# A Mamba-2 scan ahead of a hash-routed expert layer: other load pieces, another order of steps, three experts' weights on chip

## The chip, the cores and the metric

The kernel runs on one core of one Trainium2 chip. Its engines are TensorE (PE, with its weight loads as PEld), VectorE (DVE), ScalarE (ACT), GpSimd (POOL) and SyncE (SP), which here only issues transfers. The metric is the device time of one execution in microseconds, lower is better. All arithmetic is float32, apart from small tables of the routing.

## What is computed

Four batches of eight heads are scanned in chunks, and the result, 3072 tokens of 256 values, goes through one of eight experts, chosen by a hash of the token's id.

```python
# scan: x (4, 8, 768, 32), a (4, 8, 768), B and C (4, 8, 768, 16)
cum = np.cumsum(np.log(a_chunk), axis=-1)
M = einsum('bhin,bhjn->bhij', Cc, Bc) * exp(cum_i - cum_j) * causal
y = einsum('bhij,bhjd->bhid', M, xc) + einsum('bhin,bhnd->bhid', Cc, state) * exp(cum)
state = exp(sum(la)) * state + sum_j Bx * exp(cum_last - cum_j)
# experts: 3072 tokens of 256, w1 (8, 256, 1024), w2 (8, 1024, 256)
e = token_id * 2654435761 % 8
out[token] = relu(y[token] @ w1[e]) @ w2[e]
```

## The kernel before

The kernel has a prologue, a scan and an expert stage. The scan is one loop over 24 tiles `gc` of 128 tokens (L523), six tiles to a batch, and each tile holds two steps of 64 tokens, so a batch has 12 steps `k`. The order on every engine of prologue and scan is the program's (`tc.manual_schedule`, L78); in the expert stage a planner orders the work.

For a tile, `grams(gc)` (L451) multiplies B with C on PE and VectorE masks the product into `m` (L463); `outputs(gc)` (L467) adds the part from the state (`cp` by `up`, L476) and the part inside the chunk (`m` by `x`, L485), ScalarE copies it out (L489), and SyncE stores it to the scratch tensor `y_tokens` (L490). The products of a tile are made one tile ahead of its outputs.

While a batch's tiles run, the next batch is prepared by pieces, one after each tile's outputs. `rows(b, i)` (L357) scales B (i = 0) or C (i = 1) with the decays, on GpSimd for batches 1 to 3. `put_steps(b)` (L364) stores B's rows to the DRAM scratch `b_steps`; `get_steps(b)` (L367) reads them back in another layout as `bs`, by two transfers that wait for the store. `turn_b(b)` and `turn_c(b)` (L398, L404) transpose the rows on PE (L395) and copy them out of PSUM; `turn_c` makes `ct`, `cp` and the two masked copies `ce`. `states(b, half)` (L419) multiplies `bs` with `x` on PE (L431) and runs the recurrence over the steps on VectorE (L436, L438); `blocks` (L441) spreads the states into `up` on GpSimd. For batch 0 there is no trip through DRAM: `turn_steps(0)` (L375) transposes on PE instead.

For batch 1 the pieces come after tiles 0 to 4 (rows and store after 0, `turn_b` and `get_steps` after 1, `turn_c` after 2, the two halves of `states` after 3 and 4), and rows of batch 2 after tile 5. For batches 2 and 3, `turn_b` comes after tile 6 or 12, `turn_c` after 7 or 13, `states` after 8, 9 or 14, 15, and the rows and the store of batch 3 after tile 10. B and C of a batch arrive by `load_bc` (L87, two buffers), x by `load_x` (L94, two transfers, three buffers); batches 0 and 1 are asked for in the prologue, batch 2 after tiles 3 and 4, batch 3 after tiles 6 and 7. All of these, and the stores of y, stand in SyncE's one queue in program order.

The routing's many small VectorE operations are a generator (`routing`, L182): three of its parts run in the prologue (`next(todo)`, L306, L312, L499), the others one after each tile from tile 7. `spin` (L155) is PE work whose result nobody reads.

In the expert stage each expert has 416 slots. `gather` (L586) fetches token rows by an indirect transfer that GpSimd issues, `turn_x` transposes them, `up` and `down` (L607, L614) are the two products, and the results are scattered to the output. An expert's two weights take 1 MB each; `load_w` (L112) has NWB = 4 buffers. Experts 0 and 1 are loaded from ScalarE's queue after tiles 13 and 17, expert 2 from SyncE's at the end of the scan (L559), expert 3 by L625, later ones when an expert's buffers come free.

Of the kernel before, what the change touches and what calls it, by code (L numbers as in the profile page):

```python
# [20 lines left out]
def kernel(  # L21
# [21 lines left out]
    NCH = NT // P  # L43
    DP = DM // P
    FP = F // P
    NWB = 4
    CAP = 416
    KT = -(-CAP // P)
    LR = CAP - (KT - 1) * P
# [41 lines left out]
                              in_=src[b].rearrange("h (p r) n -> p h (r n)", r=RS))  # L91
        bcs[b] = t

    def load_x(b):  # L94

        t = aload.tile([P, G, NU, D], F32, name="x_t", bufs=3)
        for q in range(2):
            nc.sync.dma_start(out=t[q * HL:(q + 1) * HL].rearrange("j h k d -> j (h k) d"),
                              in_=x[b, q * G:(q + 1) * G].rearrange("h s d -> (h s) d").rearrange("(c j) d -> j c d", j=HL))
        xs[b] = t  # L100

    tok_h = dataclasses.replace(moe_token_ids.tensor, shape=list(moe_token_ids.tensor.shape))
    tok = route.tile([NCH, P, 2], I32)
# [2 lines left out]
    load_x(0)  # L106
    load_bc(1)
    load_x(1)

    w1s, w2s = {}, {}  # L110

# [43 lines left out]
    def spin(moving, n=1):  # L155

        t = ps_y.tile([P, 2, 512], F32, name="y_ps")
        for _ in range(n):
            nc.tensor.matmul(out=t[:, 0, 0:moving.shape[-1]], lhsT=ident[0:moving.shape[0]], rhs=moving,
                             start=True, stop=True)  # L160
# [141 lines left out]
    tot = cum[:, :, RS - 1]  # L302
    rel_ps = ps_t.tile([P, 512], F32, name="tp")
    nc.tensor.matmul(out=rel_ps[0:NR, 0:BH], lhsT=rel_w.rearrange("p k r -> p (k r)"), rhs=tot, start=True, stop=True)
    todo = iter(routing())
    next(todo)  # L306
    rel = apre.tile([NR, BH, RS], F32)
    nc.vector.tensor_tensor(out=rel, in0=cum, in1=rel_ps[0:NR, 0:BH].unsqueeze(2).to_broadcast([NR, BH, RS]), op=OP.add)
    fac = apre.tile([NR, 2, BH, RS], F32)
    nc.scalar.activation(fac[:, 0], rel, AF.Exp, scale=-1.0)  # L310
    nc.scalar.activation(fac[:, 1], rel, AF.Exp)
    next(todo)  # L312
    spin(flat(cum), 4)

    totx = apre.tile([NR, BH, NS], F32)
    step = const.tile([P, NB, NU], F32)
# [17 lines left out]
    def steps():  # L334
        step_ps = ps_t.tile([P, 512], F32, name="tp")
        for b in range(NB):
            nc.tensor.matmul(out=step_ps[:, b * NU:(b + 1) * NU],
                             lhsT=totx[:, b * H:(b + 1) * H].rearrange("p h n -> p (h n)"), rhs=step_w,
                             start=True, stop=True)
        nc.scalar.activation(step.rearrange("p b k -> p (b k)"), step_ps[:, 0:NB * NU], AF.Exp)  # L340
# [16 lines left out]
    def rows(b, i, eng):  # L357

        t = abat.tile([NR, RS, P], F32, name="rows", bufs=2)
        eng.tensor_tensor(out=t.rearrange("p r (h n) -> p h r n", h=H), in0=bcs[b][:, i],  # L360
                          in1=fac[:, i, b * H:(b + 1) * H].unsqueeze(3).to_broadcast([NR, H, RS, NS]), op=OP.mult)
        rws[b, i] = t

    def put_steps(b):  # L364
        nc.sync.dma_start(out=b_dram[b].rearrange("(p r) n -> p r n", r=RS), in_=rws[b, 0])

    def get_steps(b):  # L367

        t = abat.tile([P, NU, HL], F32, name="bs")
        for q in range(2):  # L370
            nc.sync.dma_start(out=t[q * HL:(q + 1) * HL],
                              in_=b_dram[b].rearrange("(k j) (q n) -> q j k n", j=HL, q=2)[q])
        bss[b] = t
# [24 lines left out]
    def turn_b(b):  # L398
        bt = abat.tile([P, NR, RS], F32, name="bt")
        for rs, v in turned(b, 0):  # L400
            nc.scalar.activation(bt[:, :, rs], v, AF.Copy)
        bts[b] = bt.rearrange("p (k c) r -> p k (c r)", c=RU)

    def turn_c(b, first=False):  # L404
        ct = abat.tile([P, NR, RS], F32, name="ct", bufs=1)
        ce = abat.tile([P, 2, NR, RS], F32, name="ce")
        for rs, v in turned(b, 1):
            nc.scalar.activation(ce[:, 0, :, rs], v, AF.Identity, scale=par[:, 0:1])
            if first:
                nc.vector.tensor_scalar(out=ce[:, 1, :, rs], in0=v, scalar1=par[:, 1:2], scalar2=None, op0=OP.mult)  # L410
            else:
                nc.scalar.activation(ce[:, 1, :, rs], v, AF.Identity, scale=par[:, 1:2])
            nc.scalar.activation(ct[:, :, rs], v, AF.Copy)
        cp = abat.tile([P, NU, HL], F32, name="cp")
        nc.gpsimd.tensor_tensor(out=cp, in0=ct.rearrange("p (k c) r -> p k (c r)", c=RU),
                          in1=step[:, b].unsqueeze(2).to_broadcast([P, NU, HL]), op=OP.mult)
        ces[b], cps[b] = ce.rearrange("p e (k c) r -> p e k (c r)", c=RU), cp
# [33 lines left out]
    def grams(gc):  # L451

        b, c = divmod(gc, R)
        gram = ps_g.tile([P, 2, 512], F32, name="gram")
        for u in range(2):
            for r in range(G):
                q, g = divmod(r, 2)
                rr = slice(32 * r, 32 * r + 32)
                nc.tensor.matmul(out=gram[q * HL:(q + 1) * HL, g, u * P:(u + 1) * P],  # L459
                                 lhsT=bts[b][rr, 2 * c + u], rhs=ces[b][rr, :, 2 * c + u],  # L460
                                 start=True, stop=True)
        m = awork.tile([P, 2, 2, 2, HL], F32, name="m")
        nc.vector.tensor_tensor(out=m.rearrange("p g u e i -> p g (u e i)"), in0=gram[:, :, 0:2 * P],  # L463
                                in1=causal.rearrange("p (g x) i -> p g (x i)", g=2), op=OP.mult)
        ms[gc] = m
# [24 lines left out]
        nc.sync.dma_start(out=y_dram[gc * P:(gc + 1) * P, :], in_=y_sb.rearrange("p q d -> p (q d)"))  # L490

    rows(0, 0, nc.vector)
    rows(0, 1, nc.vector)
    heads()
    steps()
    spin(ones, 2)
    turn_b(0)
    spin(ones, 2)
    next(todo)  # L499
    turn_c(0, True)  # L500
    turn_steps(0)
    grams(0)
    states(0, 0)
    blocks(0, 1, 2, nc.vector)
    blocks(0, 2, UH + 1, nc.gpsimd)

    def prepare(nb, what):
        if nb >= NB:
            return
        if what == "rows":  # L510
            rows(nb, 0, nc.gpsimd)
            put_steps(nb)
            rows(nb, 1, nc.gpsimd)
        elif what == "b":
            turn_b(nb)
            get_steps(nb)
        elif what == "c":
            turn_c(nb)
        else:
            states(nb, what)  # L520
            blocks(nb, *((1, UH + 1), (UH + 1, NU))[what], nc.gpsimd)

    for gc in range(NCH):  # L523
        b, c = divmod(gc, R)
        nb = b + 1
        if gc + 1 < NCH:
            grams(gc + 1)
        outputs(gc)
        if gc == 0:
            states(0, 1)  # L530
            blocks(0, UH + 1, NU, nc.gpsimd)
        if gc > 6:
            next(todo, None)
        if b == 0:
            if c in (0, 1):
                prepare(1, ("rows", "b")[c])
            elif c == 2:
                prepare(1, "c")
            elif c == 3:
                prepare(1, 0)  # L540
                load_bc(2)
            elif c == 4:
                prepare(1, 1)
                load_x(2)
            else:
                prepare(2, "rows")
        elif c < 4:
            prepare(nb, ("b", "c", 0, 1)[c])
            if c == 0 and nb + 1 < NB:
                load_bc(nb + 1)  # L550
            if c == 1 and nb + 1 < NB:
                load_x(nb + 1)
        elif c == 4:
            prepare(nb + 1, "rows")
        if gc in (13, 17):
            load_w((gc - 13) // 4, nc.scalar)
    for _ in todo:
        pass
    load_w(2, nc.sync)  # L559
    scan_order.__exit__(None, None, None)  # L560
    a_ctx.close()

# [51 lines left out]
    def down(e, f):  # L614
        if f == 0:
            oP[e] = ps_o.tile([P, DP, 512], F32, name="o_ps")
        h = hT.pop((e, f))
        for j in range(DP):
            nc.tensor.matmul(out=oP[e][:, j, 0:CAP], lhsT=w2s[e][:, f, j * P:(j + 1) * P], rhs=h,  # L619
                             start=(f == 0), stop=(f == FP - 1))  # L620
        if f == FP - 1:
            if e + NWB < E:
                load_w(e + NWB, nc.sync)
            if e == 0:
                load_w(NWB - 1, nc.sync)  # L625
            op = oP.pop(e)
            oT[e] = mwork.tile([P, DP, CAP], F32, name="oT")
            for j in range(DP):
                if j % 2 == 0:
                    nc.scalar.activation(oT[e][:, j], op[:, j, 0:CAP], AF.Copy)  # L630
                else:
                    nc.vector.tensor_copy(out=oT[e][:, j], in_=op[:, j, 0:CAP])
# [19 lines left out]
    for u in range(E * FP + LAG):  # L652
        e, f = divmod(u, FP)
        if e < E:
            up(e, f)
        if u >= LAG:
            down(*divmod(u - LAG, FP))
        if f >= FP - KT and e + 1 < E:
            turn_x(e + 1, f - (FP - KT))
            if e + 2 < E:  # L660
                gather(e + 2, f - (FP - KT))
        if LAG < f <= LAG + KT and 0 < e < E:
            turn_o(e - 1, f - LAG - 1)
# [74 lines left out]
```

## Time and profile before

| what | us |
|---|---|
| median of 3 runs | 337.86 (337.04 to 339.86) |
| the profiled execution, its own time | 338.07 |
| its span, first to last instruction | 336.3 |
| PE busy in it | 285.5 (85%) |
| POOL, DVE, ACT busy in it | 100.7, 99.8, 53.9 |
| first products of the expert stage begin at | 125.1 |

Times within the execution count from the first instruction. An entry of the timeline or of the chain gives its start, its length and its engine; "<-" in brackets names what ended the idle time before it. The granted clock is TensorE's clock as a share of 2.4 GHz, so 0.50 is 1.2 GHz. SPq, ACTq and POOLq are the sequencers that issue transfers.

### The profile page before, as it was taken

How to read it: one execution, taken by the hardware profiler on the slowest of the kernel's cores; microseconds unless marked ns; L12 is line 12 of the kernel's file. 1: busy time of each engine (PE TensorE's matmuls, PEld its weight loads, DVE VectorE, ACT ScalarE, POOL GpSimd, SP SyncE). 2: the span in 40 equal slices, each digit the busy share in tenths (PEclk: the TensorE clock that was granted, in tenths of full speed). 3: DMA queues.
4: the chain of work that ended last, by engine and by line, in shares of the span. 5: the costliest groups of instructions: out<-in, count | busy, mean ns of one | idle time of the engine just before them, and what ended most of it. 6: DMA issues, size and time to landing. Idle time of an engine off the chain costs nothing.

```text
span 336.3 us, 6038 instructions
## 1 busy us (share of the span) xinstructions
PE 285.5 (85%) x2507; PEld 180.8 (54%) x2507; DVE 99.8 (30%) x215; ACT 53.9 (16%) x116; POOL 100.7 (30%) x114
## 2 busy tenths in 40 slices
PE   6786975678968149999999999999999999999930
PEld 5765855567756125555555555555555555555510
DVE  4642245486784010212212221211211311211110
ACT  4301424003301001011201101102111111111110
POOL 6136181260410372220530531531621301302240
PEclk9957595555769558999999999999999999999975
DMA  7992496963855792043154154244200000000110
GB/s 120 154 117 63 98 159 135 206 133 96 285 175 176 241 368 76 16 160 125 55 168 125 62 165 125 78 144 135 69 20 16 30 2 16 31 0 16 35 48 1
DMA packets 55936, 35.64 MB, mean 106 GB/s; under 512 B 34464, under 2 KB 51898, under 8 KB 55909
## 3 DMA queue, kind: packets, MB, share of 16 engines
q1 hardware_dynamic: 50468, 24.51, 32.4%
q0 software_dynamic: 2816, 6.56, 6.1%
q10 hardware_dynamic: 2624, 4.19, 3.8%
q8 instruction: 20, 0.33, 0.5%
q14 instruction: 8, 0.06, 0.1%
HBM read 27.78 MB, written 7.73 MB: 106 GB/s over the span
## 4 chain that ended last, share of the span: by engine, by line
PE 51%; issue 20%; DMA 12%; DVE 7%; POOL 6%; ACT 2%; SPq 0%; POOLq 0%; ACTq 0%; DVEq 0%
PE h_ps L610 17%; PE o_ps L619 16%; DMA out_dram<-o_sb,idx_out 6%; PE gram L459 4%; POOL out_dram L580 3%; PE y_ps L485 3%; PE tp L395 2%; DMA xg<-y_tokens,idx_in 2%; PE y_ps L476 2%; PE tp L431 2%; PE xt_ps L598 2%; DVE st L438 1%; DMA bs<-b_steps 1%; POOL rows L360 1%; DMA a_t<-in_a_dram 1%
## 5 line engine op out<-in xcount | busy, mean ns | idle before, releaser
L610 PE MATMUL h_ps<-xT,w 128*128 128x416 f32 x256 | 101.8, 522 | 0.3 <-issue 0.3
L619 PE MATMUL o_ps<-hT,w 128*128 128x416 f32 x256 | 102.1, 518 | 0.0
L619 PEld LDWEIGHTS o_ps<-hT,w 128*128 128x128 f32 x256 | 47.5, 190 | 40.1 <-issue 36.3
L580 POOL DMA_INDIRECT out_dram<-o_sb,idx_out x32 | 31.2, 975 | 114.1 <-ACT o_sb L641 95.8
L610 PEld LDWEIGHTS h_ps<-xT,w 128*128 128x128 f32 x256 | 47.1, 194 | 32.3 <-issue 31.1
L575 POOL DMA_INDIRECT xg<-y_tokens,idx_in x32 | 32.0, 1001 | 54.9 <-issue 21.0
L605 DVE TENSOR_SCALAR hT<-h_ps 128x416 f32<-128x416 f32 x32 | 18.9, 592 | 74.4 <-PE h_ps L610 74.4
L599 DVE COPY xT<-xt_ps 128x256 f32<-128x256 f32 (+1 forms) x32 | 12.0, 374 | 77.2 <-PE xt_ps L598 76.7
L603 ACT ACTIVATE hT<-h_ps 128x416 f32<-128x416 f32 x32 | 16.5, 517 | 99.0 <-PE h_ps L610 81.5
L459 PE MATMUL gram<-ce,bt 32*64 32x128 f32 x384 | 24.3, 372 | 1.9 <-issue 1.9
L463 DVE TENSOR_TENSOR m<-gram,causal 128x512 f32<-128x512 f32 x24 | 16.5, 687 | 25.2 <-PE gram L459 25.2
L485 PE MATMUL y_ps<-x_t,m 64*64 64x32 f32 x768 | 20.8, 254 | 2.6 <-DVE m L463 2.0
L598 PE MATMUL xt_ps<-ident,xg 128*128 128x128 f32 (+1 forms) x64 | 12.6, 280 | 12.0 <-issue 10.1
L485 PEld LDWEIGHTS y_ps<-x_t,m 64*64 64x64 f32 x768 | 20.7, 180 | 3.8 <-DVE m L463 3.0
L598 PEld LDWEIGHTS xt_ps<-ident,xg 128*128 128x128 f32 (+1 forms) x64 | 8.5, 148 | 25.2 <-issue 22.1
L446 POOL TENSOR_TENSOR up<-st,own 128x640 f32<-128x640 f32 (+1 forms) x8 | 13.1, 1643 | 26.2 <-DVE st L438 26.2
L489 ACT ACTIVATE y_sb<-y_ps 128x256 f32<-128x256 f32 x24 | 9.2, 383 | 65.2 <-PE y_ps L485 63.1
L459 PEld LDWEIGHTS gram<-ce,bt 32*64 32x64 f32 x384 | 15.4, 181 | 5.8 <-issue 4.8
L476 PE MATMUL y_ps<-up,cp 64*64 64x128 f32 x176 | 14.2, 365 | 3.1 <-issue 1.3
L641 ACT ACTIVATE o_sb<-ot_ps 128x256 f32<-128x256 f32 x16 | 6.1, 383 | 60.2 <-PE ot_ps L638 60.2
L431 PE MATMUL tp<-x_t,bs 64*32 64x64 f32 x352 | 10.5, 290 | 6.0 <-DMA bs<-b_steps 6.0
L395 PE MATMUL tp<-ident,rows 96*128 96x96 f32 x64 | 10.3, 328 | 5.5 <-POOL rows L360 5.5
(122 smaller groups left out, 178.6 us busy)
## 6 DMA issues: line engine op xcount, KB each, us to landing
w<-in_moe_w_dram SPq DMA_DIRECT2D x12, 1024.0 KB, 5.5
w<-in_moe_w_dram ACTq DMA_DIRECT2D x4, 1024.0 KB, 5.9
x_t<-in_x_dram SPq DMA_DIRECT2D x8, 384.0 KB, 9.1
y_tokens<-y_sb SPq DMA_DIRECT2D x24, 128.0 KB, 3.2
bc<-in_B_dram SPq DMA_DIRECT2D x4, 384.0 KB, 6.8
bc<-in_C_dram SPq DMA_DIRECT2D x4, 384.0 KB, 6.1
b_steps<-rows SPq DMA_DIRECT2D x3, 384.0 KB, 3.3
bs<-b_steps SPq DMA_DIRECT2D x6, 192.0 KB, 3.7
```

The costliest lines, as they stand in the source:

```text
L395: nc.tensor.transpose(out=v[:, :, r], in_=t[:, r0 + r], identity=ident[0:NR, 0:NR])
L431: nc.tensor.matmul(out=tp[32 * r:32 * r + 32, i * PW:(i + 1) * PW], lhsT=bs[w, k, 32 * g:32 * g + 32], rhs=xb[w, 2 * g:2 * g + 2, k], star ...
L459: nc.tensor.matmul(out=gram[q * HL:(q + 1) * HL, g, u * P:(u + 1) * P], lhsT=bts[b][rr, 2 * c + u], rhs=ces[b][rr, :, 2 * c + u], start=Tr ...
L463: nc.vector.tensor_tensor(out=m.rearrange("p g u e i -> p g (u e i)"), in0=gram[:, :, 0:2 * P], in1=causal.rearrange("p (g x) i -> p g (x ...
L476: nc.tensor.matmul(out=y_ps[u * HL:(u + 1) * HL, q, 0:P], lhsT=cps[b][w, k], rhs=ups[b][w, k].rearrange("p g x -> p (g x)"), start=True, s ...
L485: nc.tensor.matmul(out=y_ps[u * HL:(u + 1) * HL, q, h * D:(h + 1) * D], lhsT=m[w, g, u, e], rhs=xs[b][w, h, k], start=(k == 0 and h == 0), ...
L575: nc.gpsimd.indirect_dma_start(out=dst, out_offset=None, in_=y_dram[:], in_offset=bass.IndirectOffsetOnAxis(ap=idx, axis=0), bounds_check= ...
L580: st = nc.gpsimd.indirect_dma_start(out=out[:], out_offset=bass.IndirectOffsetOnAxis(ap=idx, axis=0), in_=src, in_offset=None, bounds_chec ...
L598: nc.tensor.transpose(out=tp[:, i, 0:r], in_=g[0:r, i * P:(i + 1) * P], identity=ident[0:r, 0:r])
L605: nc.vector.tensor_scalar_max(out=o, in0=i, scalar1=0.0)
L610: nc.tensor.matmul(out=hp, lhsT=w1s[e][:, i, f * P:(f + 1) * P], rhs=xT[e][:, i], start=(i == 0), stop=(i == DP - 1))
L619: nc.tensor.matmul(out=oP[e][:, j, 0:CAP], lhsT=w2s[e][:, f, j * P:(j + 1) * P], rhs=h, start=(f == 0), stop=(f == FP - 1))
```

## The change

- `load_x` takes a piece number: x of batches 2 and 3 is asked for in four pieces of two heads, each by two transfers (one a head, 96 KB instead of 384 KB), after tiles 1 to 4 (batch 2) and 6 to 9 (batch 3). Batches 0 and 1 stay whole.
- B and C of batch 2 are asked for at the end of the prologue's loads, those of batch 3 after tile 6.
- B's rows of batch 1 are made ahead of the tile loop, behind `blocks(0, 2, ...)` on GpSimd, and C's rows after tile 0. For batches 2 and 3 B's rows are made after tile 4 or 9, ahead of that tile's `blocks`, and the store and C's rows come after tile 5 or 10.
- In the prologue, the routing's first part comes behind the decays, its second ahead of `turn_c`, its third behind the first `grams`; `steps` and `turn_b(0)` come ahead of `rows(0, 1)`; two of the spins go and one is shortened.
- In `turn_c` for batch 0, ScalarE copies `ct` out of PSUM, and both `ce` are made from that copy in SBUF, in two halves of positions, one mask on ScalarE and one on VectorE.
- NWB is 3. Expert 2 is loaded from ScalarE's queue in the expert stage, behind the second `up`; the loads at L559 and L625 go.

```diff
-    NWB = 4
+    NWB = 3
+    def load_x(b, i=None):
+        if i in (None, 0):
+            xs[b] = aload.tile([P, G, NU, D], F32, name="x_t", bufs=3)
+        for h in range(*((0, H, G) if i is None else (2 * i, 2 * i + 2))):
+            q, g = divmod(h, G)
+            n = G if i is None else 1
+            nc.sync.dma_start(out=xs[b][q * HL:(q + 1) * HL, g:g + n].rearrange("j h k d -> j (h k) d"),
+                              in_=x[b, h:h + n].rearrange("h s d -> (h s) d").rearrange("(c j) d -> j c d", j=HL))
     load_x(1)
+    load_bc(2)
...
-    todo = iter(routing())
-    next(todo)
     rel = apre.tile([NR, BH, RS], F32)
...
     nc.scalar.activation(fac[:, 1], rel, AF.Exp)
+    todo = iter(routing())
     next(todo)
-    spin(flat(cum), 4)
+    spin(flat(cum), 3)
...
         for rs, v in turned(b, 1):
             nc.scalar.activation(ct[:, :, rs], v, AF.Copy)
+            if not first:
+                for e in range(2):
+                    nc.scalar.activation(ce[:, e, :, rs], v, AF.Identity, scale=par[:, e:e + 1])
+        for p in range(0, NR, NR // 2) if first else ():
+            ps = slice(p, p + NR // 2)
+            nc.scalar.activation(ce[:, 0, ps], ct[:, ps], AF.Identity, scale=par[:, 0:1])
+            nc.vector.tensor_scalar(out=ce[:, 1, ps], in0=ct[:, ps], scalar1=par[:, 1:2], scalar2=None, op0=OP.mult)
...
     rows(0, 0, nc.vector)
+    steps()
+    turn_b(0)
     rows(0, 1, nc.vector)
     heads()
-    steps()
-    spin(ones, 2)
-    turn_b(0)
-    spin(ones, 2)
     next(todo)
     turn_c(0, True)
     turn_steps(0)
     grams(0)
+    next(todo)
     states(0, 0)
     blocks(0, 1, 2, nc.vector)
     blocks(0, 2, UH + 1, nc.gpsimd)
+    rows(1, 0, nc.gpsimd)
     for gc in range(NCH):
...
+        b, c = divmod(gc - (b == 0), R)
+        nb = max(b, 0) + 1
+        after = nb + 1
+        if nb == NB:
+            continue
+        if gc == 0:
+            put_steps(1)
+            rows(1, 1, nc.gpsimd)
+        elif c == 0:
+            turn_b(nb)
+            get_steps(nb)
+            if nb == 2:
+                load_bc(3)
+        elif c == 1:
+            turn_c(nb)
+        elif c == 2:
+            states(nb, 0)
+            blocks(nb, 1, UH + 1, nc.gpsimd)
+        elif c == 3:
+            states(nb, 1)
+            if after < NB:
+                rows(after, 0, nc.gpsimd)
+            blocks(nb, UH + 1, NU, nc.gpsimd)
+        elif c == 4 and after < NB:
+            put_steps(after)
+            rows(after, 1, nc.gpsimd)
+        if after < NB and gc > 0 and c < 4:
+            load_x(after, c)
         if gc in (13, 17):
             load_w((gc - 13) // 4, nc.scalar)
...
-    load_w(2, nc.sync)
...
-            if e == 0:
-                load_w(NWB - 1, nc.sync)
...
             up(e, f)
+        if u == 1:
+            load_w(NWB - 1, nc.scalar)
```

## Rows read from the trace of the kernel before

**Rows 1.** Windows: start:end, length, busy time (and instructions) by engine, granted clock, DMA, GB/s
```profile
23.50:39.40 15.90, 12.48 (x262) 10.66 (x262) 3.91 (x9) 4.88 (x11) 6.86 (x5) 0.61 0.32 78
39.40:61.90 22.50, 14.14 (x389) 11.47 (x385) 9.63 (x29) 5.92 (x14) 9.86 (x6) 0.73 0.78 146
...
110.90:125.10 14.20, 2.43 (x8) 1.15 (x8) 1.50 (x4) 0.00 (x0) 9.06 (x9) 0.50 0.96 326
125.10:322.00 196.90, 196.18 (x626) 107.65 (x626) 38.85 (x82) 26.05 (x54) 50.38 (x52) 0.99 0.23 73
```

**Rows 2.** Waits of PE between 21 and 111 us: total, times, longest
```profile
PE tp L431 <- DMA bs<-b_steps: 6.0, 2, 5.5
PE tp L395 <- POOL rows L360: 5.5, 2, 3.4
```

**Rows 3.** Chain of work that ended last, 20 to 64 us: start, length, what
```profile
53.67 3.27 DMA b_steps<-rows
...
57.66 4.19 DMA bs<-b_steps
```

**Rows 4.** Timeline of SyncE's queue: start, length of the issue, transfer
```profile
13.44 5.97 SPq L98 DMA_DIRECT2D x_t<-in_x_dram  x2
...
43.47 6.50 SPq L98 DMA_DIRECT2D x_t<-in_x_dram  x2
50.06 3.51 SPq L490 DMA_DIRECT2D y_tokens<-y_sb  x1
```

**Rows 5.** Windows in which x of batch 1, then B and C of batch 2, move
```profile
21.40:23.90 2.50, 1.34 (x25) 0.97 (x28) 2.31 (x8) 0.00 (x0) 0.60 (x1) 0.50 1.25 102
23.90:25.50 1.60, 1.60 (x55) 1.54 (x52) 0.12 (x1) 0.38 (x1) 0.94 (x1) 0.50 0.10 18
...
43.00:47.00 4.00, 3.26 (x109) 2.52 (x108) 3.00 (x8) 0.77 (x2) 3.76 (x3) 1.00 1.03 222
```

**Rows 6.** Timeline of GpSimd: `up` of batches 0 and 1, rows of batch 2
```profile
23.30 1.54 POOL L446 TENSOR_TENSOR up<-st,own 128x640 f32<-128x640 f32 x1 [4.49 <-DVE st L438]
...
42.91 1.81 POOL L446 TENSOR_TENSOR up<-st,own 128x768 f32<-128x768 f32 x1 [2.25 <-DVE st L438]
...
46.47 3.81 POOL L360 TENSOR_TENSOR rows<-bc,fac 96x1024 f32<-96x1024 f32 x2
```

**Rows 7.** Windows cut where the granted clock changes
```profile
40.80:50.90 10.10, 7.75 (x257) 6.16 (x255) 5.16 (x15) 2.02 (x5) 7.13 (x4) 1.00 0.82 145
...
61.90:88.40 26.50, 23.95 (x496) 19.51 (x496) 18.14 (x35) 6.03 (x14) 8.91 (x5) 0.50 0.74 156
88.60:95.30 6.70, 4.83 (x192) 3.79 (x188) 6.49 (x12) 0.77 (x2) 2.97 (x2) 1.00 0.59 202
...
102.20:108.90 6.70, 5.53 (x213) 4.50 (x208) 3.57 (x9) 1.53 (x4) 0.00 (x0) 1.00 0.45 150
```

**Rows 8.** Timeline of ScalarE: a tile's copy out, at the lower and higher clock
```profile
74.56 0.38 ACT L489 ACTIVATE y_sb<-y_ps 128x256 f32<-128x256 f32 x1 [2.16 <-PE y_ps L485]
...
...
104.74 0.38 ACT L489 ACTIVATE y_sb<-y_ps 128x256 f32<-128x256 f32 x1 [1.06 <-PE y_ps L485]
```

**Rows 9.** Chain between scan and experts: start, length, what
```profile
115.17 6.70 DMA xg<-y_tokens,idx_in
...
124.39 0.42 PE xt_ps L598 x2
```

**Rows 10.** Timeline: fourth gather of expert 0
```profile
117.78 0.94 POOL L575 DMA_INDIRECT xg<-y_tokens,idx_in  x1 [0.31 <-issue]
```

**Rows 11.** Windows behind one later gather, issued at 139.2 us
```profile
140.00:141.00 1.00, 1.00 (x4) 0.52 (x4) 0.59 (x1) 0.00 (x0) 0.22 (x1) 1.00 0.11 20
141.00:142.00 1.00, 1.00 (x6) 0.61 (x5) 0.02 (x1) 0.00 (x0) 0.00 (x0) 1.00 0.34 111
```

**Rows 12.** Chain in the prologue, `turn_c(0)`: start, length, what
```profile
13.86 0.59 ACT ce L408
...
16.77 0.50 ACT ct L413
```

More of the change, by code (lines that the diff above doesn't have):

```diff
@@ L92, in load_bc @@
         bcs[b] = t
[L94 to L100, printed above, removed]
+    def load_x(b, i=None):
[6 more added lines that the diff above has]
+                              in_=x[b, h:h + n].rearrange("h s d -> (h s) d").rearrange("(c j) d -> j c d", j=HL))
     tok_h = dataclasses.replace(moe_token_ids.tensor, shape=list(moe_token_ids.tensor.shape))
@@ L407, in turn_c @@
         for rs, v in turned(b, 1):
[L408 to L412, printed above, removed]
-            nc.scalar.activation(ct[:, :, rs], v, AF.Copy)
+            nc.scalar.activation(ct[:, :, rs], v, AF.Copy)
+            if not first:
[5 more added lines that the diff above has]
+            nc.vector.tensor_scalar(out=ce[:, 1, ps], in0=ct[:, ps], scalar1=par[:, 1:2], scalar2=None, op0=OP.mult)
         cp = abat.tile([P, NU, HL], F32, name="cp")
@@ L505 @@
     blocks(0, 2, UH + 1, nc.gpsimd)
[L507 to L521, printed above, removed]
+    rows(1, 0, nc.gpsimd)
     for gc in range(NCH):
         b, c = divmod(gc, R)
-        nb = b + 1
         if gc + 1 < NCH:
@@ L533 @@
             next(todo, None)
[L534 to L554, printed above, removed]
+        b, c = divmod(gc - (b == 0), R)
[26 more added lines that the diff above has]
+            load_x(after, c)
         if gc in (13, 17):
```

## The prediction

> **What bounds the kernel now.** I read the windows by stage first, then TensorE's waits in the scan, then the chain of work around the longest of them, and last the queue that feeds that chain. In the expert stage the reader is to see one number: PE is busy 196.18 of 196.90 us [rows 1]. That stage is PE's own work, the change takes no product out of it, so everything has to be won ahead of 125.1 us. There PE is not full: 12.48 of 15.90 us from 23.5 to 39.4, where the states of batch 1 begin, and 14.14 of 22.50 from there to 61.9, where those of batch 2 begin [rows 1].
>
> The waits name two causes: `bs` back from DRAM, 6.0 us in 2 times, and the rows made on GpSimd, 5.5 us in 2 times, the longest 3.4 [rows 2]. The chain shows the first as a trip: the store of B's rows leaves at 53.67 and takes 3.27, the read-back leaves at 57.66 and takes 4.19, so PE may go on at 61.9 [rows 3]. The trip starts late. The rows themselves were ready at 46.47 + 1.9 = 48.4 (half of the pair that lasts 3.81) [rows 6]. But SyncE was issuing x of the next batch from 43.47 for 6.50 us, and the store of y behind it needed 3.51 more, until 53.57 [rows 4]. So 5.2 us of the trip's delay are SyncE's queue. Between scan and experts a third place shows: the second gather of token rows takes 6.70 us [rows 9], while 326 GB/s flow [rows 1]; 326 GB/s by 14.2 us are 4.6 MB, four of them weights of experts 2 and 3, asked for at the scan's end.
>
> **Part by part.** *Prologue.* In `turn_c(0)` six copies of one PSUM tile each follow one another from 13.86 to 17.3, 3.4 us [rows 12]. Two of `ct` at 0.5 and then two halves of `ce` at 0.6, on two engines side by side, make 2.2, so 1.2 less; the transposes ahead of it may come earlier too, but the mask product of the routing now stands between. The third routing part now lies between VectorE's work on the first products and on the states. I estimate 0 to 2.7 us for all of it, as an estimate from these rows, and show next why I book none.
>
> *States of batch 1.* B's rows of batch 1 now follow the first `up` on GpSimd, which ended at 23.30 + 1.54 = 24.8; with 1.9 they end at 26.8 or earlier [rows 6], so the transposes of `turn_b(1)` no longer wait (3.4 us). What is late next is the trip of batch 1. Its store is queued behind B and C of batch 2, a load that the change puts ahead of it: SyncE is done with x of batch 1 at 13.44 + 5.97 = 19.4 [rows 4], the packets of x flow until about 23.9 (DMA share 1.25, then 0.10), and B and C take 4.0 us at 222 GB/s [rows 5]. That gives 27.9, about 0.5 for the store of y, 3.3 for the store of rows, 0.7 to issue the read and 4.2 for it [rows 3]: 36.6. If the store passes B and C, rows at 24.8 plus the same trip give 33.0. PE by itself needs its 12.48 us from 23.5, 36.0, or up to 2.7 less with the prologue's gain. I take 35.8, near the queue's value because transfers of one queue have followed each other here: 3.6 us earlier than 39.4, with bounds of 2.8 and 6.4. The prologue's gain lies under this wait.
>
> *States of batch 2.* From the states of batch 1 to the end of the `up` that follows is 44.72 - 39.40 = 5.3 us; the rows stood behind a second `up` and are now ahead of it: 1.9 [rows 6], then 0.3 to issue, 3.3, 0.7 and 4.2 for the trip [rows 3], 15.7 in all. x now comes in pieces that were asked for earlier, so SyncE reaches the store after one store of y. The second `up` comes 1.9 us later and is first read at tile 9, so it is hidden by three tiles. PE's own work in this stretch is 14.14 us at the clock of before; 7.75 of it ran at the higher clock [rows 7], and a tile at the lower costs 2.16 + 0.38 = 2.54 against 1.06 + 0.38 = 1.44 us, a factor of 1.76 [rows 8], so all at the lower level it is 20.0. Between 15.7 and 20.0 I take 16.6, since before the clock was high for most of it. Against 22.5 that is 5.9 less (bounds 2.5 and 6.8). The second wait for rows, 2.1 us, is inside this.
>
> *Batch 3 and the tail.* From 61.9 to 110.9 no wait for `bs` or rows is left; the same instructions run in the same order, apart from rows one tile earlier. I book 0, with 3 lost to 6 gained, by the clock.
>
> *The gathers.* Expert 2's weights now stand behind the first relu in ScalarE's queue, expert 3's behind expert 0's end. A gather issued at 139.2, with no weights moving, brought its 131 KB by 142.0 (20 GB/s, then 111, in a microsecond each): 2.8 us [rows 11]. The fourth gather is issued at 117.78 [rows 10], so its rows would be there at 120.6; the transpose and copy then take 125.1 - 124.4 = 0.7 [rows 9], and the products start at 121.4 in place of 125.1: 3.7 less, with 1.8 as the lower bound if ScalarE issues the load early and half the weights still meet the gathers.
>
> *Three buffers.* An expert lasts 196.9 / 8 = 24.6 us. Expert 2's load is asked for some 49 us ahead of use, and each later one two experts ahead, about 49 us; 2 MB at the 326 GB/s of [rows 1] is 6.4. Cost nothing; without that cover it would be at most 6.4 an expert.
>
> **The sum.** 3.6 + 5.9 + 0 + 3.7 = 13.2. The profiled execution took 338.07 with a span of 336.3, so 1.8 lies outside; the median of the runs is 337.86, nearly the same. 336.3 - 13.2 + 1.8 = 324.9: I predict 325.
>
> **Rivals.** *The pieces of x cost more than the whole.* There are now eight transfers of 96 KB a batch instead of two, on the queue that the trip uses. If each cost as much as one lone transfer of 131 KB, 2.8 us [rows 11], they would fill 22.4 us from about 32 to 54, and the store of rows (due near 43) would wait up to 10: the 5.9 are gone, 331. Against it: the trip's two read transfers leave 0.6 us apart and are both there after 4.19 [rows 3], so lengths overlap. The Trainium skill, page "DMA: Bandwidth & Descriptors", section "Anatomy of one DMA", speaks for this rival: a transfer has a fixed cost of about 2.0 us (measured there for another kind of queue). By it, eight would be an estimated 17.8 us a batch and the end near 330; no row here shows such pieces.
>
> *The clock stays high.* It was at the lower level from 61.9 to 88.4, with PE busy 23.95 of 26.5 us and VectorE 18.14 [rows 7]. Should PE, with shorter waits ahead of it, keep 2.4 GHz there, PE's part shrinks to 23.95 / 1.76 = 13.6 and VectorE's 18.1 carries it: up to 8.4 more, I say 6: 319. Against it: a wait of one or two us ahead of the states of batch 2 remains, and before, the level fell within such stretches.
>
> *The clock is lost.* The stretches at the higher level, 40.8 to 50.9, 88.6 to 95.3 and 102.2 to 108.9, held 7.75 + 4.83 + 5.53 = 18.1 us of PE work [rows 7]. PE now waits ahead of the states of batch 1, and spins are gone. If all three fall to the lower level, that costs 18.1 x 0.76 = 13.8, a little more than the 13.2: 339, slower than before. It decides from the point where all of them are lost; for losing one I see some ground, for all three little.
>
> **How the numbers follow.** The forecast (320 to 329) gets 0.52. The high clock (313 to 320) 0.17, the costly pieces (329 to 334) 0.18, the lost clock 0.13, of which 0.09 within 1% and 0.04 beyond. A measurement of this kernel can tell about 1%, 3.4 us, from no change. So faster 0.87, same 0.09, slower 0.04. The range 314 to 332 leaves out the lost clock and the ends of the two others.
>
> **What would show it.** Right: no wait of `turn_b` for GpSimd's rows; the states of batch 1 near 36 and of batch 2 near 52; the store of batch 2's rows issued within a microsecond of their end; the last tile near 101; second gather about 3 us, and 10.5 us from the last tile's copy to the first product instead of 14.2; expert stage 197 us as before. Wrong: a wait for `bs` ahead of batch 2 as long as before with x packets ahead of the store; PE waiting for weights; a granted clock at the lower level in stretches that had the higher.

## The result

The changed kernel takes 328.18 us (median of 4 runs, 327.07 to 329.3) against 337.93: a ratio of 0.9704, interval 0.965 to 0.9758. The forecast was 325 us with a range of 314 to 332. The profiled execution took 327.07 with a span of 325.3, 11.0 less than before. Ratios and intervals in this document leave out executions more than 1.5% above a kernel's fastest (single ones took 373, 471 and 919 us), so they are not quite the quotients of the medians.

The windows of the changed kernel, cut at the same events as [rows 1] (first outputs, begin of the states of batches 1, 2 and 3, last tile's copy, first product of the experts), with the same columns:

```profile
23.70:35.50 11.80, 11.75 (x260) 10.07 (x260) 3.89 (x9) 4.89 (x11) 7.59 (x5) 0.57 0.78 179
35.50:53.00 17.50, 12.44 (x390) 10.30 (x384) 10.60 (x29) 5.83 (x14) 9.19 (x6) 0.89 0.62 133
53.00:76.90 23.90, 21.55 (x436) 17.53 (x437) 17.79 (x32) 5.66 (x13) 8.36 (x5) 0.50 0.60 126
76.90:103.40 26.50, 20.92 (x600) 17.47 (x596) 16.47 (x28) 3.80 (x10) 3.71 (x3) 0.76 0.81 283
103.40:114.40 11.00, 2.40 (x8) 1.15 (x9) 1.50 (x4) 0.04 (x1) 6.15 (x6) 0.50 0.22 67
114.40:311.00 196.60, 195.81 (x628) 107.66 (x628) 38.88 (x82) 26.07 (x54) 53.26 (x55) 0.99 0.25 82
```

| stretch | before, us | after, us | forecast | measured |
|---|---|---|---|---|
| start to first outputs | 23.6 | 23.7 | 0 | +0.1 |
| to the states of batch 1 | 15.8 | 11.8 | -3.6 | -4.0 |
| to the states of batch 2 | 22.5 | 17.5 | -5.9 | -5.0 |
| to the states of batch 3 | 24.0 | 23.9 | 0 | -0.1 |
| to the last tile's copy | 24.9 | 26.5 | 0 | +1.6 |
| to the first product of the experts | 14.3 | 11.0 | -3.7 | -3.3 |
| to the end | 211.2 | 210.9 | 0 | -0.3 |
| sum | 336.3 | 325.3 | -13.2 | -11.0 |

In the first stretch shown PE is busy 11.75 of 11.80 us, where 12.48 of 15.90 stood [rows 1]: in this execution the states of batch 1 wait for hardly anything but PE's own work. In the second, PE is still idle for 5 us of 17.5. PE's waits between 15 and 105 us (who waited for whom, total, times, longest) say for what:

```profile
PE y_ps L489 <- DVE m L467: 4.3, 3, 2.0
PE tp L435 <- DMA bs<-b_steps: 4.1, 2, 3.1
...
PE tp L397 <- POOL rows L362: 1.0, 1, 1.0
```

The wait for rows fell from 5.5 us to 1.0, that for `bs` only from 6.0 to 4.1 [rows 2]. SyncE's timeline around batch 2's trip, and GpSimd's:

```profile
40.25 2.18 SPq L101 DMA_DIRECT2D x_t<-in_x_dram  x2
42.53 0.59 SPq L494 DMA_DIRECT2D y_tokens<-y_sb  x1
43.21 0.37 SPq L367 DMA_DIRECT2D b_steps<-rows  x1
43.68 0.39 SPq L494 DMA_DIRECT2D y_tokens<-y_sb  x1
48.24 1.29 SPq L373 DMA_DIRECT2D bs<-b_steps  x2
...
40.85 1.93 POOL L362 TENSOR_TENSOR rows<-bc,fac 96x1024 f32<-96x1024 f32 x1
```

The rows end at 42.78 and the store leaves 0.4 us later, where 5.3 us lay between them before [rows 4, 6]. The store takes 3.4 us, to 46.6, but the read-back leaves only at 48.24. SyncE's own waits between 40 and 60 us name what it waited for:

```profile
SPq L665 <- DVE one_ub L231: 3.3, 1, 3.3
```

L665 is `values_load(nov)`, written near the end of the program: SyncE reads the count of overflow tiles from SBUF into a register there. The planner had put it into SyncE's queue between tile 6's store of y and batch 2's read-back. The count is computed in the routing's part after tile 7. The kernel before had the same read in that place (its L672), but there it hardly showed. Its SyncE waits between 54 and 57 us:

```profile
SPq L371 <- DMA b_steps<-rows: 0.9, 1, 0.9
SPq L672 <- DVE val L236: 0.8, 1, 0.8
```

SyncE waited 0.9 us more for the store to land after it had read the count, so there the landing was the later of the two.

### The profile page after: what moved, and what is told of

Its sections match the earlier page's. It is cut to its first block, busy times and chain, and to the rows that moved or that the text cites. A ratio compares the mean times of both kernels' runs of the same rounds, so it can differ in the third digit from the quotient of the medians.

```text
span 325.3 us, 6033 instructions
## 1 busy us (share of the span) xinstructions
PE 283.6 (87%) x2497; PEld 180.3 (55%) x2497; DVE 102.9 (32%) x215; ACT 54.1 (17%) x116; POOL 101.6 (31%) x114
## 3 DMA queue, kind: packets, MB, share of 16 engines
q0 software_dynamic: 2816, 6.56, 6.3%
## 4 chain that ended last, share of the span: by engine, by line
PE 51%; issue 20%; DMA 10%; DVE 9%; POOL 6%; ACT 1%; POOLq 0%; SPq 0%; DVEq 0%; ACTq 0%
PE h_ps L603 17%; PE o_ps L612 16%; DMA out_dram<-o_sb,idx_out 6%; PE y_ps L489 3%; POOL out_dram L573 3%; PE tp L397 3%; PE gram L463 3%; DVE st L442 2%; PE xt_ps L591 2%; PE y_ps L480 2%; DMA bs<-b_steps 1%; PE tp L435 1%; DMA a_t<-in_a_dram 1%; PE ot_ps L629 1%; POOL up L450 1%
## 5 line engine op out<-in xcount | busy, mean ns | idle before, releaser
L596 ACT ACTIVATE hT<-h_ps 128x416 f32<-128x416 f32 x32 | 16.6, 517 | 95.0 <-PE h_ps L603 95.0
L489 PE MATMUL y_ps<-x_t,m 64*64 64x32 f32 x768 | 21.5, 255 | 6.9 <-DVE m L467 4.3
L463 PE MATMUL gram<-ce,bt 32*64 32x128 f32 x384 | 22.2, 359 | 0.2 <-DVE m L467 0.2
L450 POOL TENSOR_TENSOR up<-st,own 128x640 f32<-128x640 f32 (+1 forms) x8 | 13.2, 1644 | 22.1 <-DVE st L442 22.0
L463 PEld LDWEIGHTS gram<-ce,bt 32*64 32x64 f32 x384 | 14.3, 173 | 3.1 <-issue 1.7
L629 PE MATMUL ot_ps<-ident,oT 128*128 128x128 f32 (+1 forms) x64 | 12.5, 281 | 1.5 <-ACT o_sb L632 0.7
L419 POOL TENSOR_TENSOR cp<-ct,step 128x768 f32<-128x768 f32 x4 | 6.2, 1552 | 23.3 <-ACT ct L410 23.3
```

The costliest lines, as they stand in the source:

```text
L450: eng.tensor_tensor(out=ups[b][:, k0:k1], in0=sts[b][:, k0:k1].unsqueeze(2).to_broadcast(sh), in1=own.rearrange("p g e d -> p g (e d)").un ...
L489: nc.tensor.matmul(out=y_ps[u * HL:(u + 1) * HL, q, h * D:(h + 1) * D], lhsT=m[w, g, u, e], rhs=xs[b][w, h, k], start=(k == 0 and h == 0), ...
L596: nc.scalar.activation(o, i, AF.Relu)
```

## Experiments

The theory was that three things won the time, each by itself: rows that no longer wait on GpSimd, a trip through DRAM that leaves earlier, and gathers without weights beside them. The rivals were that the order of rows alone does it and the pieces of x nothing, that the weights are beside the point, and that the read of `nov` and expert 2's load hold back more than is seen.

### The weights alone, the scan alone

`weights_only` is the kernel before with

```diff
-    NWB = 4
+    NWB = 3
...
-    load_w(2, nc.sync)
...
-            if e == 0:
-                load_w(NWB - 1, nc.sync)
...
+        if u == 1:
+            load_w(NWB - 1, nc.scalar)
```

and `scan_only` is the changed kernel with these lines as before.

> The kernel before with the weights part of the change alone (three buffers, expert 2 from ScalarE's queue, nothing asked for at the scan's end). If the gathers of expert 0 were late because 4 MB of weights moved beside them, the second gather takes about 3.0 us instead of 6.7, the first product follows the last tile's copy by 11.0 us instead of 14.3, and the time is 3.3 us lower, 334.6 (ratio 0.990). If the gathers are slow for another reason (the read of rows just stored), the 14.3 us stay and the ratio is 1.00. In the changed kernel the planner put expert 2's load into the scan's last tiles, not behind the first relu; if that load is what makes those tiles 1.6 us longer there, the stretch from the states of batch 3 to the last copy grows here too, from 24.9 to about 26.5, and only half of the 3.3 is left.

> The changed kernel with the weights as before (four buffers, experts 2 and 3 asked for at the scan's end). If the parts add up, the states of batch 1 begin near 35.6 and those of batch 2 near 53.0 as in the changed kernel, and the time is the kernel before less 8.8, 329.1, or 327.5 if the last tiles also lose their extra 1.6 us; the gathers are slow again (14.3 us from last copy to first product). If the weights part brought nothing, this equals the changed kernel, 328.2.

Measured: `weights_only` 333.94 us, ratio 0.9903 (0.985 to 0.9956). From the last copy to the first product it takes 10.5 us. `scan_only` took 331.13 us, ratio 0.9834 (0.9788 to 0.988), and the product of the two ratios, 0.974, agrees with the 0.9704 of both together. Its states of batches 1 and 2 begin at 35.7 and 53.0, as in the changed kernel, and its gathers are slow again. The chain between scan and experts, first of `scan_only`, then of the changed kernel (start, length, what):

```profile
109.66 6.23 DMA xg<-y_tokens,idx_in
115.88 0.14 issue
116.02 0.68 PE xt_ps L592 x2
```

```profile
106.73 3.00 DMA xg<-y_tokens,idx_in
109.73 0.14 issue
109.86 0.67 PE xt_ps L591 x2
```

The gather on this chain is the second of expert 0 in the first two cases: 6.70 us before [rows 9], 6.23 in `scan_only`. In the changed kernel it is the first, 3.00 us, and the gathers of that stretch take 2.4 to 3.6 us from issue to landing. The two kernels differ in the weights alone, so that the weights slowed the gathers is shown. In `scan_only` the stretch from the states of batch 3 to the last copy lasts 27.9 us, with no load of expert 2 in it. That does not clear the load, since this execution had a granted clock of 0.62 there against 0.76 in the changed kernel; `behind_relu` below is the better test.

### The pieces of x, three times

`x_pieces_only` gives the kernel before the new `load_x` and asks for x of batch 2 after tiles 1 to 4 and of batch 3 after 6 to 9. `x_whole` takes the pieces out of the changed kernel, and `nov_x_whole`, run later, does the same to `nov_late` below:

```diff
-        if after < NB and gc > 0 and c < 4:
-            load_x(after, c)
+        if gc in (4, 7):
+            load_x(2 if gc == 4 else 3)
```

> The kernel before with x of batches 2 and 3 asked for in pieces after tiles 1 to 4 and 6 to 9, and nothing else. If SyncE's queue held up the store of batch 2's rows for 5.2 us, the store now leaves when the rows are ready (48.4 to 48.8 instead of 53.7), PE gets bs about 5 us earlier (states of batch 2 near 57 instead of 61.9) and the time is 333 (ratio 0.985). If the place of the rows on GpSimd is what matters, the store leaves no earlier than before and the ratio is 1.00. If pieces cost more on the queue than two whole transfers, the store leaves later than 53.7 and the ratio is above 1.00.

> The changed kernel with x of batches 2 and 3 asked for whole, after tiles 4 and 7 as before, everything else as changed. If SyncE's queue was what delayed the store of batch 2's rows, the store again leaves 4 to 5 us after the rows' end (42.8), the states of batch 2 begin near 57 instead of 53, and the time is 332. If the earlier place of the rows carries the gain and the pieces none, as pieces alone brought no gain (ratio 0.9998), the store leaves at 43.2 as in the changed kernel and the time stays at 328.

> nov_late with x of batches 2 and 3 asked for whole after tiles 4 and 7. In x_whole the store left 2.7 us after the rows' end and took 4.7 us instead of 3.4, yet the read-back left only 0.5 us later than in the changed kernel, because there it stood behind the read of nov. With that read out of the way the pieces should show their worth: rows' end to bs landed near 11.8 us instead of 8.2, states of batch 2 about 3 us later than in nov_late, time 328. If the pieces are worth nothing, the time equals nov_late's, 325.

Measured: pieces alone 337.4 us, ratio 0.9998 (0.9944 to 1.0052), so nothing; the changed kernel without them 328.26 us, ratio 0.9797 (0.9748 to 0.9847), where 332 stood in the theory; `nov_x_whole` 329.94 us, ratio 0.9788 (0.973 to 0.9846), against 324.48 and 0.9643 (0.9567 to 0.9719) for `nov_late_again` on the same chip. SyncE's timeline of `x_pieces_only`, `x_whole` and `nov_x_whole`:

```profile
52.29 0.37 SPq L367 DMA_DIRECT2D b_steps<-rows  x1
...
56.99 0.59 SPq L373 DMA_DIRECT2D bs<-b_steps  x1
```

```profile
37.84 4.02 SPq L101 DMA_DIRECT2D x_t<-in_x_dram  x2
41.96 1.96 SPq L494 DMA_DIRECT2D y_tokens<-y_sb  x1
44.01 0.38 SPq L367 DMA_DIRECT2D b_steps<-rows  x1
...
48.74 1.29 SPq L373 DMA_DIRECT2D bs<-b_steps  x2
```

```profile
40.11 3.81 SPq L101 DMA_DIRECT2D x_t<-in_x_dram  x2
44.02 3.80 SPq L494 DMA_DIRECT2D y_tokens<-y_sb  x1
47.92 0.38 SPq L367 DMA_DIRECT2D b_steps<-rows  x1
...
51.27 1.28 SPq L373 DMA_DIRECT2D bs<-b_steps  x2
```

How long the store waits behind its rows follows what stands ahead of it in SyncE's queue: 0.6 us with pieces alone (51.7 to 52.29), 2.7 us in `x_whole` (rows at 41.3) and 4.8 us in `nov_x_whole` (43.1) with x whole. What that is worth depends on the rest. In `x_whole` the read-back left as the store landed, at 48.74. In the changed kernel it left at 48.24, because there it stood behind `nov` and the early store was partly wasted: from the states of batch 1 to those of batch 2 it is 18.5 us in `x_whole` (34.7 to 53.2) against 17.5, or 16.8 to 18.0 in the four profiles with earlier rows, pieces and that read. The times do not say more: 328.26 equals the changed kernel's 328.18, but it was measured on another chip, and by the ratios (0.9797 against 0.9704, intervals that just overlap) the pieces are worth up to 3 us there. With `nov` out of the way they are worth 5.5 us by the medians, and the same stretch is 20.1 us without them (35.9 to 56.0) against 15.8 in `nov_late_again` (34.6 to 50.4).

In `x_pieces_only` the rows themselves came 3.3 us later than before (51.7 against 48.4), since they still stood behind the second `up`:

```profile
45.57 1.81 POOL L448 TENSOR_TENSOR up<-st,own 128x768 f32<-128x768 f32 x1 [3.63 <-DVE st L440]
48.24 1.54 POOL L448 TENSOR_TENSOR up<-st,own 128x640 f32<-128x640 f32 x1 [0.86 <-DVE st L440]
49.74 3.82 POOL L362 TENSOR_TENSOR rows<-bc,fac 96x1024 f32<-96x1024 f32 x2
```

Those 3.3 us are hardly the pieces' doing: its first outputs began 1.3 us later than before and the store of batch 1 took 4.8 us instead of 3.3, both before the first piece was issued at 38.84, so that the `bs` of batch 1 came 2.6 us late. Why its ten runs show no gain at all, with the store's wait gone, the trace suggests. SyncE's waits between 52.5 and 57 us:

```profile
SPq L675 <- DVE one_ub L230: 2.7, 1, 2.7
SPq L373 <- DMA b_steps<-rows: 0.3, 1, 0.3
```

The read of `nov` (L675 here, the count being written at 55.54) held the queue until 0.3 us before the store landed, so in this execution an even earlier store would have brought the read-back forward by 0.3 us at most. The count, too, came 3.4 us later than before. This is read from the trace; no run takes the read of `nov` out of `x_pieces_only`. Nor was the rows' earlier place run alone.

### The read of the count

```diff
-        nc.vector.tensor_copy(out=nov, in_=tend[:, E - 1:E])
...
         nc.vector.tensor_scalar(out=idx_in, in0=idx_out, scalar1=float(NT - 1), scalar2=None, op0=OP.min)
+        nc.vector.tensor_copy(out=nov, in_=tend[:, E - 1:E])
```

> The changed kernel with the copy of the routing's count nov moved from tile 7's part to the last part. SyncE reads that count into a register, and the planner had put this read between tile 6's store and the read-back of batch 2's steps. If that read is what holds the read-back from 46.6 (the store landed) to 48.2, it now leaves at 46.6 to 46.8, the states of batch 2 begin near 51.4 instead of 53.0, and the time falls by 1.6, to 326.6. If the read-back waits for something else, its start stays at 48.2 and the time at 328.2.

> The same kernel as nov_late (the changed kernel with the copy of nov in the last routing part), as the level that the three others of this chip are compared with. 325.1, ratio 0.966 to the kernel before; read-back of batch 2 within 0.2 us of the store's landing.

Measured: 325.13 us, ratio 0.966 (0.9607 to 0.9713), and on another chip 324.48, ratio 0.9643. The intervals overlap the changed kernel's, so the time alone would not settle it; the queue does. SyncE's timeline of `nov_late_again`:

```profile
42.08 0.38 SPq L367 DMA_DIRECT2D b_steps<-rows  x1
42.55 0.39 SPq L494 DMA_DIRECT2D y_tokens<-y_sb  x1
45.47 1.28 SPq L373 DMA_DIRECT2D bs<-b_steps  x2
```

The read-back leaves 0.1 us after the store has landed (45.33), not 1.6. In `nov_late` the states of batch 1 began at 34.3 and those of batch 2 at 49.8, 15.5 us where the changed kernel needs 17.5. In this and the three profiles nearest to it (`nov_late_again`, `nov_behind`, `nov_pre_late`) it is 15.5 to 16.3, against 16.8 to 18.0 in the changed kernel and its nearest (`scan_only`, `old_prologue`, `behind_relu`). (The states begin with four products that need only the first of the two `bs` transfers; as in the table, the begin counted is that of the rest.)

### The trip earlier

`trip_early` is `nov_late` with expert 2's load held behind the first relu (that much is `nov_behind` below), and

```diff
             turn_c(nb)
+            if after == 2:
+                rows(2, 0, nc.gpsimd)
         elif c == 2:
+            if after == 2:
+                put_steps(2)
             states(nb, 0)
```

with the read-back of batch 2 after tile 5; batch 3 is as in the changed kernel.

> nov_behind with the rows of B of batch 2 made right after tile 2 on GpSimd, their store after tile 3 and the read-back after tile 5, so that the trip through DRAM lies well ahead of its use. If the trip from the states of batch 1 by up, rows, store and read sets the begin of the states of batch 2 (15.5 us in nov_late against a forecast of 15.7), that stretch now falls to PE's own work, 13 to 14 us, there is no wait for bs ahead of batch 2, and the time is 1.5 to 2.5 below nov_behind, about 322. If PE's own work already sets it, nothing changes.

Measured: 321.55 us (320.3 to 324.16), ratio 0.956 (0.9491 to 0.9629), the fastest of all. PE's waits between 30 and 60 us, first of `nov_late_again`, then of `trip_early`:

```profile
PE tp L435 <- DMA bs<-b_steps: 4.0, 3, 2.1
PE tp L435 <- ACT ce L413: 1.3, 1, 1.3
PE tp L397 <- POOL rows L362: 1.2, 2, 0.8
```

```profile
PE gram L463 <- issue: 2.1, 1, 2.1
PE tp L435 <- ACT ce L413: 1.2, 1, 1.2
PE tp L435 <- DMA y_tokens<-y_sb: 0.5, 1, 0.5
```

The states of batch 2 begin 13.9 us after those of batch 1 (35.7 to 49.5), 2.1 less than the 16.0 of `nov_behind` (35.6 to 51.6), which differs from it in the trip alone. So up to there the trip had set that stretch, and its 2.1 us are most of the 2.9 between the medians. The 13.9 are not PE's own work alone: PE is busy for 12.14 of 13.86 us. No wait is put down to `bs` any more, but its two transfers, issued at 44.35 and 44.98, took 4.2 and 4.4 us and landed about when the products on them began (48.64 and 49.51), so the trip is still close.

### Expert 2's load and the prologue

`behind_relu` changes the changed kernel, `nov_behind` does the same to `nov_late`:

```diff
-            load_w(NWB - 1, nc.scalar)
+            with tc.issue_after(relus[0].ins):
+                load_w(NWB - 1, nc.scalar)
```

(`relus` collects the relus in program order; `issue_after` holds an issue behind an instruction.)

> The changed kernel with expert 2's load held behind the first relu in ScalarE's queue, where the program has it; the planner had put it at 90 to 95 us, in the scan's last tiles. If its 2 MB there lengthen the last tiles, the stretch from the states of batch 3 to the last copy falls from 26.5 to 25 us, while the gathers keep their 11.0 us, and the time is 326.6. If that stretch is set by the granted clock and VectorE, it stays at 25 to 28 and the time at 328; if the load now meets the gathers of expert 1, which are issued in the same microseconds, nothing waits for those before expert 1 and the time is the same.

> nov_late with expert 2's load held behind the first relu. If the 2 MB in the scan's last tiles cost anything, as the run behind_relu leaves open (326.2), the stretch from the states of batch 3 to the last copy is 1 to 2 us shorter than in nov_late_again and the time 323.5 to 324. If they cost nothing, 325.

ScalarE's timeline of the changed kernel shows where the planner had put the load, and that of `behind_relu` that it moved:

```profile
90.37 0.39 ACT L493 ACTIVATE y_sb<-y_ps 128x256 f32<-128x256 f32 x1 [2.12 <-PE y_ps L489]
90.40 0.37 ACTq L117 DMA_DIRECT2D w<-in_moe_w_dram  x1
94.58 0.39 ACT L493 ACTIVATE y_sb<-y_ps 128x256 f32<-128x256 f32 x1 [3.82 <-PE y_ps L489]
94.60 0.37 ACTq L119 DMA_DIRECT2D w<-in_moe_w_dram  x1
```

```profile
116.78 0.52 ACT L596 ACTIVATE hT<-h_ps 128x416 f32<-128x416 f32 x1 [14.27 <-PE h_ps L603]
116.81 0.38 ACTq L117 DMA_DIRECT2D w<-in_moe_w_dram  x1
```

Measured: 326.22 us, ratio 0.9722 (0.9669 to 0.9774), and 324.49 us, ratio 0.9623 (0.9566 to 0.968). Neither can be told from the kernel it was made from (0.9704 and 0.9643). The stretch from the states of batch 3 to the last copy lasts 25.6 and 27.1 us, against 26.5 in the changed kernel and 26.4 in `nov_late_again`: the load's place costs nothing that shows. The first product follows the last copy by 11.0 us in both, as it does in the changed kernel, so either place leaves expert 0's gathers free.

`old_prologue` gives the changed kernel the prologue of before, with its order, spins and masks. `nov_pre_late` is `nov_late` with the routing's third part behind batch 0's first `up`:

```diff
     grams(0)
-    next(todo)
     states(0, 0)
     blocks(0, 1, 2, nc.vector)
+    next(todo)
```

> The changed kernel with the prologue's order, spins and masks for batch 0 as before. My forecast booked nothing for this part because the states of batch 1 were to wait for their trip anyhow; the changed kernel's first outputs began at 23.7, before at 23.6, so the part brought nothing by itself either. Then first outputs near 23.6, states of batch 1 near 35.6, time 328 (within 2 us). If the new prologue is worth its 1 to 2.7 us and only the low clock of that one profile hid it, first outputs are 1 to 2 us later than in the other runs with the new prologue (21.8 to 23.7) and the time is 329 to 330.

> The changed kernel with the count's copy nov in the last routing part (as in nov_late) and with the routing's third part moved on VectorE from ahead of batch 0's recurrence to behind its first up. The third part took 1.1 us between the first mask product and the recurrence, so first outputs should begin 1 us earlier. If the states of batch 1 wait for their trip, half or less of that is left, since the rows of batch 1 follow the first up; expected 324 to 325, and about 1 below nov_late. If the trip hides it all, 325.1 as nov_late.

Measured: `old_prologue` 326.81 us, ratio 0.9741 (0.966 to 0.9822), and `nov_pre_late` 325.45, ratio 0.9683 (0.9599 to 0.9768): no difference from 0.9704 and 0.966. First outputs began at 26.6 in the one and 21.0 in the other, 5.6 us apart, and the states of batch 1 at 37.4 and 34.7: more than half of what the prologue wins or loses is gone again by the states of batch 1. The expected 23.6 for the old order was wrong by 3 us in that profile. With the new order first outputs lay between 21.0 and 23.7 in the profiles of this study, so the new order may bring 1 to 3 us there; the total does not show it.

## Why the prediction was right

**The bound.** The expert stage was left as it was, 195.81 us of PE work in 196.60 against 196.18 in 196.90 [rows 1], and all but 0.3 of the 11.0 us came from ahead of it.

**States of batch 1: right in size, for half the reason.** Forecast 35.8, measured 35.5. But I let the store's place behind B and C of batch 2 set it. The store left with the rows' end, at 26.93, and the read-back at 29.98, 3.0 us later, where I had 3.3 and a queue until 28.4 ahead of it; `bs` was there at about 35.0 (its second transfer was issued at 30.64 and took 4.4 us), half a microsecond ahead of use. That is the trip without the queue, for which I had 33.0 by a slip: I added the trip to 24.8, where the `up` ends and the rows begin, and not to their end at 26.8, which gives 35.0. So the bound of 6.4 us should have been 4.4. PE's own work set the begin, which I had counted at 33.3 to 36.0. In `behind_relu`, the same up to there, PE waited 2.5 us for `bs` ahead of these states. The bounds all lie between 33.3 and 36.6, so that the value held is in part luck.

**States of batch 2: the mechanism right, one wait not seen.** I had 15.7 for the trip, and took 16.6, the 0.9 us more for the clock. The stretch measured 15.5 to 16.3 once `nov` was out of the way (`nov_late` and its kin), and 17.5 with it. The missing term, 1.6 us between the store's landing and the read-back, was in front of me: it stood in the kernel's last lines and in SyncE's waits of the kernel before (0.8 us), because the planner had moved the read into the scan, whose order I had taken to be the program's alone. The clock was granted at 0.89 there, so the 0.9 us were not needed for it and covered half of the term by luck. `trip_early` shows that the trip, and not PE, set the stretch.

**The queue's 5.2 us: a diagnosis that stood half.** I read the delay as SyncE's alone. Pieces of x alone won nothing, taken out of the changed kernel they cost about 1 us of the stretch, and out of `nov_late` 5.5 us of the time. The waits do not add up, they run side by side and the later one counts: the store waits for its rows and for its turn in the queue, the read-back for the store and for the read of `nov`. In the kernel before the count was written at 52.17; the changed kernel's read-back left 1.2 us after the count (47.08 to 48.24), and by that, an estimate, the read-back of before could have left at 53.3 instead of 57.03, which is 3.7 of the 5.2 us. In the changed kernel the count came sooner, 11.5 us behind the begin of the states of batch 1 where it had been 12.8, and the rows left GpSimd sooner too. So the sum came near because more than the queue was moved.

**The pieces' price.** The rival of costly pieces fell: x of batch 2 was issued from 32.12 to 42.4 in eight pieces, and the store left 0.4 us after its rows. A pair of pieces took SyncE 1.3 to 2.2 us to issue, and a piece landed a median 3.5 us after its issue, so their lengths overlap. The Trainium skill ("DMA: Bandwidth & Descriptors", section "Anatomy of one DMA") gives a fixed cost of about 2.0 us a transfer. Over the pieces here it did not add up.

**Batch 3 and the tail.** Forecast 0 with -6 to +3; measured +1.5, all of it in the last stretch. From the states of batch 2 to those of batch 3 it is 23.9 against 24.0, at 0.50 of the clock in both. The last stretch took 24.4 to 25.5 us in the four profiles with the old prologue and masks (the kernel before, `weights_only`, `x_pieces_only`, `old_prologue`) and 24.6 to 28.1, on average 26.6, in the ten with the new. So the 1.6 us seem to go with that part of the change, and my premise that the same instructions run in the same order was wrong: `turn_c` now copies `ct` ahead of the two `ce` for every batch, and VectorE is busy 16.5 to 16.6 us in this stretch in all ten, 15.6 in the four. How that would lengthen the stretch is not shown. Among the ten its length mostly follows PE's idle time that ends with nothing the profile shows, from 0.6 us in `trip_early` (24.6) to 3.3 in `nov_late` (28.1); `scan_only` has none, but the lower clock. In the changed kernel the clock was at 0.50 from 86.9 to 93.6 with PE busy throughout.

```profile
80.10:86.80 6.70, 3.87 (x157) 2.97 (x151) 6.56 (x10) 0.77 (x2) 3.35 (x2) 1.00 0.74 258
86.90:93.60 6.70, 6.70 (x122) 5.75 (x125) 3.66 (x4) 0.77 (x2) 0.00 (x0) 0.50 0.66 211
93.80:100.40 6.60, 4.88 (x196) 4.05 (x188) 3.07 (x9) 1.15 (x3) 0.00 (x0) 1.00 1.06 390
```

Above (the changed kernel's windows, cut where the granted clock changes): in the first, VectorE is busy 6.56 of 6.70 us and PE 3.87, so PE waits for VectorE at the higher clock; the level then falls, and 6.70 us of PE work run at the lower.

**The gathers.** Forecast 3.7 less (its terms, 120.6 + 0.7, give 3.8), measured 3.3, and 3.8 in `weights_only`. The price of a gather without weights, 2.8 from [rows 11], was 3.0 for the one on the chain. The gathers began half a microsecond later behind the last copy, 3.3 us (103.4 to 106.73) against 2.8 in `weights_only`. One premise failed without harm: expert 2's load did not stand behind the first relu. The planner moved it to 90.40 and 94.60, ahead of the gathers, and it was over by the time they came: from 105 to 106 us nothing moves (0 GB/s), and the first gather is issued at 106.73.

**Rivals.** The clock did not stay high from 52.8 to 80.0 (0.50), nor was it lost: 39.2 to 52.6 ran at 1.00, 13.4 us where 10.1 did [rows 7]. Three buffers cost nothing: PE is busy for all but 0.8 us of the expert stage.

## What to carry to other kernels

Where a chain goes through several queues, walk it link by link and write down what stands ahead of each link on its queue, the program's last lines included, if a planner may move them. Where a link waits for two things side by side, only the later one costs, and removing it pays only down to the other. So test an edit alone and also taken out of the whole: here the same pieces of x were worth nothing alone and 5.5 us once `nov` was out of the way. And look for loads of the next stage that run beside the transfers which lead to it: moving 4 MB out of the way of eight gathers was a cheap 3.3 us of the change.

## What was not expected of the hardware and the planner

A register read that the program has in its last block stood in SyncE's queue at 44 to 48 us and cost 1.6 us of a trip that had nothing to do with it. One operation of the routing on VectorE (`at`) took 1.90 us where it began during GpSimd's `cp` (changed kernel, 76.17) and 0.95 where it began first (before, 85.25); there `cp` took 1.79 instead of 1.47. A load written into the expert stage was issued from ScalarE's queue in the scan, 27 us ahead of the relu that it follows in the program (90.40 against 117.63). A store of 384 KB took between 3.0 and 5.1 us in the profiles of this study; the trip's length has that spread in it.
